# A fused attention and two-MoE kernel: key maxima of two batches by a GpSimd all-reduce, logits turned by transposes

## Chip, cores and metric

The kernel runs on one core of one Trainium2 chip. The metric is the device time of one execution in microseconds (us), from the core's own profile timestamps. Engines are named as in the profile: PE is TensorE (PEld its weight loads), DVE is VectorE, ACT is ScalarE, POOL is GpSimd, SP is the engine that issues most transfers. A name with q (POOLq) is an engine's own queue: instructions that steer and don't compute.

## What is computed

Linear attention with two softmaxes, then a gated MLP, then a mixture of eight experts weighted by an eight-step Sinkhorn iteration. Everything is in float32. The parts that the change touches are the second and third line of the first function (the maximum of k over the sequence) and the first line of the third.

```python
def attention(q, k, v):                    # 4 batches, 8 heads, 576 rows, 64 columns
    q_s = softmax(q, axis=-1)
    k_s = k - np.max(k, axis=2, keepdims=True)      # over the 576 rows of a head
    k_s = np.exp(k_s); k_s /= k_s.sum(axis=2, keepdims=True) + 1e-09
    kv = np.einsum('bhsd,bhse->bhde', k_s, v)
    return np.einsum('bhsd,bhde->bhse', q_s, kv)

def gated_mlp(x, w_gate, w_val, w_out, rms_g):      # 2304 x 512, inner width 1536
    xn = x / rms(x) * rms_g
    g = xn @ w_gate
    return (g * sigmoid(g) * (xn @ w_val)) @ w_out

def experts(x, w_gate, w1, w2):                     # 8 experts, inner width 1024
    logits = x @ w_gate; P = np.exp(logits - logits.max())
    for _ in range(8):
        P /= P.sum(1, keepdims=True) + 1e-9
        P /= P.sum(0, keepdims=True) + 1e-9
        P *= N / E
    return sum(P[:, e:e+1] * (np.maximum(x @ w1[e], 0) @ w2[e]) for e in range(E))
```

## The kernel before

Float32 products are split: each operand is a high part and a low part, and three matmuls (high with high, high with low, low with high) make one product. `mm3` (lines 786 to 790) issues them; the third, on line 790, reads the weight's low part, `w(1)`.

**Batches and ticks.** The attention of batch 0 is written out in `FIRST` (line 24). The attention of batches 1 to 3 is laid under the MLP products of the batch before: the loop at line 1974 goes over MLP blocks and batches, and in the first block (four slices f of the inner width) each batch b has 24 ticks. At a tick `att_do` issues the steps that the table `PLANS` (line 31) names for it. A negative tick of batch a is one of batch a-2's block: tick -5 of batch 2 is tick 19 of batch 0's block, -1 is its tick 23. Slice f has eight w_gate and w_val products, four ticks in all, and later four w_out products, two ticks. The w_out products of a slice come two slices behind the others (`LAG`), so the block of batch 0 ends with those of f=2 and f=3. There is no scheduler: every engine takes its instructions in the order in which the code issues them, and waits on semaphores.

**Weights of the MLP** are loaded raw and split by three steps, `split_a` to `split_c`, which a tick `s` in the table drives. The last of them copies the high part on ScalarE (line 370) and subtracts it on GpSimd (line 372) to get the low part; for the first twelve halves (`LO_POOL`) GpSimd does that. The last of these is the second half of w5, which is w_out of f=2 and f=3; the half itself is that of f=3. It is issued by the `s` of batch 1 at tick 20 of batch 0's block. The low half of each inner activation h is also made on GpSimd (line 837).

**Keys.** Steps `km` (`att_kmax`) take the maximum of a batch's keys over what lies in one partition, with three VectorE operations into `m1` (512 columns: 8 heads of 64). Step `mT` (`att_kmax2`) turns `m1` with four transposes and reduces it on VectorE, step `mb` (`att_kmax3`) turns the result back with four transposes of a broadcast column, so that a bank holds the maxima in every partition; ScalarE copies it to `m2`, which GpSimd reads. Steps `ks` subtract (VectorE for the main part, `G` for the 64-row tail on GpSimd), `ke` are exponentials on ScalarE, and `kv` is the product of keys and values, which begins with the tails. Steps `qm` take the query maxima on VectorE and subtract them on GpSimd (line 498), `qe` are their exponentials.

**Logits.** `logits` (line 875) leaves for each of four groups of 128 input columns eight rows of logits at partitions 32c to 32c+7 of a tile `lt`. `logits_out` (line 896) adds the four groups and turns them to token rows with one matmul a tile of 128 tokens against a 0/1 matrix `gather` (built once, line 2031), and copies the result to `probs`. There are 18 such tiles. The Sinkhorn iteration that follows uses GpSimd's `partition_all_reduce` nine times, on one and on eight columns (lines 914 and 931).

Of the kernel before, what the change touches and what calls it, by code (L numbers as in the profile page):

```python
# [7 lines left out]
F32 = mybir.dt.float32  # L8
# [4 lines left out]
ALU = mybir.AluOpType  # L13
AX = mybir.AxisListType
P = 128
# [37 lines left out]
    },  # L53
    2: {
        -6: "km_V_0 km_V_1",
        -4: "km_V_3",
        -3: "qm_0",
        -1: "mT",
        0: "qe_0",
        1: "mb ks_3_G qm_1 ks_0_V",  # L60
        2: "ke_0 ks_1_V ke_3 qT_0_0_V qT_0_1_V",
# [12 lines left out]
        22: "xT_2",  # L74
    },
    3: {
        -6: "qm_0 km_V_0",
        -5: "qm_1 km_V_1",
        -4: "km_V_3",
        -1: "mT",  # L80
        0: "mb qe_0",
        1: "ks_0_V",
        2: "ke_0 ks_3_G ks_1_V",
# [37 lines left out]
def kernel(  # L121
# [14 lines left out]
    nc = tc.nc  # L136
    B, H, S, D = q.shape
# [3 lines left out]
    E, _, F = moe2_w1.shape  # L141
    KC = DM // P
    HP = H // 2
# [19 lines left out]
    const = ctx.enter_context(tc.tile_pool(name="const", bufs=1))  # L163
# [14 lines left out]
    def psum(name):  # L178
        return pp.tile([P, 512], F32, tag="ps", name=name)

    ident = const.tile([P, P], F32, name="ident")
# [6 lines left out]
    for z in range(7):  # L188
        n = 1 << z
        nc.vector.tensor_scalar(  # L190
            out=ident[:, n : 2 * n], in0=ident[:, 0:n], scalar1=float(n), scalar2=None, op0=ALU.add
# [7 lines left out]
    probs = const.tile([P, NTILE, E], F32, name="probs")  # L199
# [2 lines left out]

    gcol = const.tile([P, KC], F32, name="gcol")

    gather = const.tile([P, E], F32, name="gather")
    xw = att[0]
    km, ms = (xp.tile([P, 1024], F32, tag=f"xt{z}", name=f"km{z}") for z in range(2))
    m1, m2 = (ms[:, z * 512 : (z + 1) * 512].rearrange("p (h d) -> p h d", h=H) for z in range(2))
# [166 lines left out]
    def split_tick():  # L375

        nb, nc_ = len(step_b), len(step_c)
        if nb:
            split_b()
        if nc_:  # L380
            split_c()
        if state["a"] < len(parts):
            if parts[state["a"]][0] < state["room"]:
                split_a()
        elif not nb and not nc_:
            pass_tick()
# [9 lines left out]
    kvn, kvd, rks, mxs, mbs = {}, {}, {}, {}, {}  # L396
# [11 lines left out]
            eng.tensor_tensor(out=m1[s, h], in0=m1[s, h], in1=ktl[s, g, h], op=ALU.max)  # L408

    def att_kmax2(b):  # L410
        mT = psum(f"mT{b}")
        for j in range(HP):
            nc.tensor.transpose(
                mT[:, j * P : (j + 1) * P], m1[:, 2 * j : 2 * j + 2, :].rearrange("p h d -> p (h d)"), ident
            )
        mxs[b] = mp.tile([P, HP], F32, tag="mx", name=f"mx{b}")
        nc.vector.tensor_reduce(
            out=mxs[b], in_=mT.rearrange("p (j s) -> p j s", j=HP), axis=AX.X, op=ALU.max
        )

    def att_kmax3(b):
        mb = psum(f"mb{b}")
        for j in range(HP):
            nc.tensor.transpose(mb[:, j * P : (j + 1) * P], mxs[b][:, j : j + 1].to_broadcast([P, P]), ident)
        mbs[b] = {nc.vector: mb.rearrange("p (h d) -> p h d", h=H).unsqueeze(2)}
        if b > 0:
            nc.scalar.copy(out=m2.rearrange("p h d -> p (h d)"), in_=mb)
            mbs[b][nc.gpsimd] = m2.unsqueeze(2)
        kvn[b] = vt[b].rearrange("p h u d -> p h (u d)")[:, :, DV : 3 * DV]
        rks[b] = mp.tile([P, H], F32, tag="rk", name=f"rk{b}")  # L430

# [360 lines left out]
    def ntok(b):  # L792
        return 512 if b < B else 256
# [46 lines left out]
    def m1_s2(f, b, h, py, first, last, tick):  # L840
        n = ntok(b)
        if f < BLOCKS[0][1]:
            split_until("o", f)
            w = wt["o", f - f % 2]
        else:
            pass_until(JOBS.index(("o", f - f % 2)) + 1)
            w = o_view(Wo[f - f % 2])
        for j in range(KC):
            mm3(
                py[j][:, 0:n],  # L850
                lambda z: w[:, z, f % 2, j * P : (j + 1) * P],
                None,
                None,
                [h[:, 0, 0:n], h[:, 1, 0:n]],
                n,
                first,
                last,
            )
            if j % 2:
                tick()  # L860
# [35 lines left out]
    def logits_out(b, pt=None):  # L896
        n = ntok(b)
        lt = lts.pop(b)
        if pt is None:
            pt = psum(f"lT{b}")  # L900
        m = n // P
        for i in range(m):
            nc.tensor.matmul(
                pt[:, i * E : (i + 1) * E], lhsT=lt[:, i * P : (i + 1) * P], rhs=gather, start=True, stop=True
            )
        nc.vector.tensor_copy(
            out=probs[:, 4 * b : 4 * b + m, :], in_=pt[:, 0 : m * E].rearrange("p (i e) -> p i e", e=E)
        )

    def sinkhorn():  # L910
# [37 lines left out]
    pt = {(p, name): dp.tile([P, 2048], F32, name=f"pt{p}{name}") for p in range(2) for name in ("T2", "T3", "T4")}  # L948
# [149 lines left out]
    def pass_tick():  # L1098

        k = state["job"]  # L1100
        if k >= min(state["jobs"], len(JOBS)):
            return
        job = JOBS[k]
        if k not in running:
            if job[0] != "t" and job not in job_raws:
                load_job(job)
                return
            after = lambda: load_job(JOBS[k + 1]) if k + 1 < len(JOBS) else None
            running[k] = (pair_sums if job[0] == "t" else convert)(job, after)
        if next(running[k], job) is job:  # L1110
            state["job"] += 1
# [862 lines left out]
    for t, (f0, f1) in enumerate(BLOCKS):  # L1974
        FT = f1 - f0
        for place, b in enumerate(range(NB) if t == 0 else (3, 2, 4)):

            now = {}
            if t == 0:
                state["tick"] = 0  # L1980
                for a, plan in PLANS.items():
                    for i, steps in plan.items():
                        i += 24 * (a - 1 - b)
                        if 0 <= i and (i < 24 or b == B - 1):
                            now[i] = now.get(i, []) + [(a, x) for x in steps.split()]

            def tick(now=now, t=t, b=b, place=place):
                for a, x in now.pop(state["tick"], ()):
                    att_do(a, x)
                state["tick"] += 1  # L1990
                if t == 0 and (b, state["tick"]) in GATES:
                    state["jobs"] = GATES[b, state["tick"]]
                if state["tick"] % 2 and not t == b == 0:
                    split_tick()
                elif EXTRA(t, b, place) and state["a"] == len(parts) and not step_b and not step_c:
                    pass_tick()

            pys = {}
            for fi in range(FT):
                f = f0 + fi  # L2000
                h = m1_s1(f, b, tick)

                def s2(f=f, b=b, h=h, fi=fi, t=t, pys=pys, tick=tick, FT=FT):
                    if fi == 0:
                        pys[0] = [psum(f"y{t}_{b}_{j}") for j in range(KC)]
                    m1_s2(f, b, h, pys[0], fi == 0, fi == FT - 1, tick)
                    if fi == FT - 1:
                        m1_evac(t, b, pys[0])

                queue.append(s2)  # L2010
                drain(LAG)
                if t == b == 0 and fi == 0:
                    load_kv(2)
                if t == b == 0 and fi == 2:
                    load_q(2, 0)
                    load_q(2, 4)
                if t > 0 and fi == 1:
                    state["jobs"] = ROOM[place]
                    if place == 0:
                        for name in ("T2", "T3", "T4"):  # L2020
                            recall_t(0, name)
            if t == 0 and b < B - 1:
                drain(0)
            if t == 0:
                assert not now, sorted(now)
                if b == 0:
                    load_q(3, 0)
                    load_q(3, 4)
                    load_kv(3)
                elif b == 2:  # L2030
                    nc.vector.tensor_reduce(
                        out=gather, in_=ident.rearrange("p (q e) -> p e q", e=E), axis=AX.X, op=ALU.add
                    )
                    state["room"] += 3
                    state["ahead"] = RAWS
                    for _ in range(RAWS - 2):
                        load_w()
# [61 lines left out]
    for z in range(2):  # L2099
        bank = psum(f"yt{z}")  # L2100
        for f in PASS:
            w = o_view(Wo[f - f % 2])
            s = slice((f - F0) * 256, (f - F0 + 1) * 256)
            for j in (0, 1):
                for i, (wz, hz) in enumerate(((0, 0), (0, 1), (1, 0))):
                    nc.tensor.matmul(
                        bank[:, j * 256 : (j + 1) * 256],
                        lhsT=w[:, wz, f % 2, (2 * z + j) * P : (2 * z + j + 1) * P],
                        rhs=h4[1 + hz][:, s],
                        start=(f == F0 and j == i == 0),  # L2110
                        stop=(f == F1 and i == 2),
# [123 lines left out]
    flat = [acc[b].rearrange("p a n -> p (a n)") for b in range(NB)]  # L2235
# [128 lines left out]
    for n in range(PER, last + 1):  # L2364
        g, e, u = units[n]
        start = n % PER == 0
# [89 lines left out]
```

## Time and profile before

| what | value |
|---|---|
| median of 3 runs | 1972.69 us (1972.36 to 1973.5) |
| profiled execution, its own time | 1972.83 us |
| its span, first to last instruction | 1971.0 us |
| instructions | 29247 |
| TensorE busy | 1947.1 us, 99% |
| VectorE busy | 1625.6 us, 82% |
| ScalarE busy | 830.0 us, 42% |
| GpSimd busy | 97.8 us, 5%, 100 instructions |
| moved by the transfer queues | 481.20 MB, mean 244 GB/s |

The attention and the first MLP block take the first 230 us or so, the logits stand near 470 and 532 us, and the rest is the experts. GpSimd works almost only in the first 280 us. In a row of a timeline the first column is the start, the second the length, and the brackets at its end tell how long the engine had been idle and what released it.

### The profile page before, as it was taken

How to read it: one execution, taken by the hardware profiler on the slowest of the kernel's cores; microseconds unless marked ns; L12 is line 12 of the kernel's file. 1: busy time of each engine (PE TensorE's matmuls, PEld its weight loads, DVE VectorE, ACT ScalarE, POOL GpSimd, SP SyncE). 2: the span in 40 equal slices, each digit the busy share in tenths (PEclk: the TensorE clock that was granted, in tenths of full speed). 3: DMA queues.
4: the chain of work that ended last, by engine and by line, in shares of the span. 5: the costliest groups of instructions: out<-in, count | busy, mean ns of one | idle time of the engine just before them, and what ended most of it. 6: DMA issues, size and time to landing. Idle time of an engine off the chain costs nothing.

```text
span 1971.0 us, 29247 instructions
## 1 busy us (share of the span) xinstructions
PE 1947.1 (99%) x10875; PEld 1810.7 (92%) x10875; DVE 1625.6 (82%) x3222; ACT 830.0 (42%) x1633; POOL 97.8 (5%) x100
## 2 busy tenths in 40 slices
PE   7899999999999999999999999999999999999999
PEld 6788888887888889999989999999999999999998
DVE  8868787755588877777778999999998989989898
ACT  5643545534355544455543333333343333333332
POOL 4521210000000000000000000000000000000000
PEclk9999999999999999999999999999999999999999
DMA  9401346587389777987787777667666767667663
GB/s 278 139 1 66 127 150 229 221 323 289 129 294 333 288 296 273 350 317 293 286 300 267 265 266 256 254 261 265 256 239 246 282 263 260 254 257 267 265 243 115
DMA packets 153974, 481.20 MB, mean 244 GB/s; under 512 B 17112, under 2 KB 81768, under 8 KB 149224
## 3 DMA queue, kind: packets, MB, share of 16 engines
q1 hardware_dynamic: 153304, 479.21, 66.7%
q8 instruction: 85, 1.39, 0.3%
q14 instruction: 57, 0.47, 0.1%
q10 hardware_dynamic: 528, 0.13, 0.0%
HBM read 334.65 MB, written 144.65 MB: 243 GB/s over the span
## 4 chain that ended last, share of the span: by engine, by line
PE 91%; DVE 4%; DMA 2%; ACT 1%; POOL 1%; issue 1%; SPq 1%; ACTq 0%; DVEq 0%; POOLq 0%
PE sb L1584 35%; PE sb L1830 13%; PE yb L1830 10%; PE yb L1619 4%; PE yb L1618 4%; PE yb L1617 4%; PE cx L1155 3%; PE cz L1155 2%; PE cy L1155 1%; PE ct L1230 1%; PE y L788 1%; PE y L790 1%; PE y L789 1%; PE pv L788 1%; PE pv L790 1%; PE pv L789 1%
## 5 line engine op out<-in xcount | busy, mean ns | idle before, releaser
L1584 PE MATMUL sb<-op1T,u 128*128 128x384 f32 x1536 | 298.4, 335 | 0.1
L1847 DVE TENSOR_TENSOR acc<-sb,acc 128x384 f32<-128x384 f32 x480 | 260.6, 557 | 27.4 <-PE sb L1830 23.2
L1584 PEld LDWEIGHTS sb<-op1T,u 128*128 128x128 f32 x1536 | 269.2, 188 | 1.1 <-DVE fx L1774 0.7
L1584 PE MATMUL sb<-op1B,u 128*128 128x384 f32 x1120 | 220.4, 335 | 0.0
L1584 PEld LDWEIGHTS sb<-op1B,u 128*128 128x128 f32 x1120 | 196.2, 188 | 0.9 <-DVE fx L1774 0.7
L1584 PE MATMUL sb<-op0T,u 128*128 128x384 f32 x768 | 149.6, 335 | 0.9 <-DVE cs L1659 0.9
L1584 PEld LDWEIGHTS sb<-op0T,u 128*128 128x128 f32 x768 | 135.6, 188 | 7.9 <-DVE cs L1659 2.5
L1774 DVE TENSOR_TENSOR fx<-mt,sb 128x384 f32<-128x384 f32 x128 | 71.0, 555 | 52.8 <-ACT mt L1778 31.2
L1584 PE MATMUL sb<-op0B,u 128*128 128x384 f32 x576 | 111.5, 336 | 0.0
L1584 PEld LDWEIGHTS sb<-op0B,u 128*128 128x128 f32 x576 | 101.5, 188 | 4.3 <-issue 1.7
L1830 PE MATMUL sb<-hc,u 128*128 128x384 f32 x504 | 104.6, 335 | 0.1
L1830 PE MATMUL sb<-hd,u 128*128 128x384 f32 x492 | 102.1, 334 | 0.1
L1830 PE MATMUL yb<-hd,u 128*128 128x384 f32 x426 | 96.7, 334 | 0.0
L1830 PEld LDWEIGHTS sb<-hc,u 128*128 128x128 f32 x504 | 88.7, 188 | 0.9 <-DVE acc L1847 0.6
L1830 PEld LDWEIGHTS sb<-hd,u 128*128 128x128 f32 x492 | 86.6, 188 | 0.7 <-ACT acc L1845 0.5
L1778 ACT COPY mt<-sb 128x384 f32<-128x384 f32 x64 | 30.8, 481 | 109.9 <-PE sb L1584 109.9
L1619 PE MATMUL yb<-u,hq 128*128 128x512 f32 x192 | 76.2, 397 | 0.3 <-DVE hq L1605 0.3
L1830 PEld LDWEIGHTS yb<-hd,u 128*128 128x128 f32 x426 | 75.9, 188 | 0.0
L1618 PE MATMUL yb<-u,hw 128*128 128x512 f32 x192 | 75.6, 394 | 0.0
L1619 PE MATMUL yb<-u,hw 128*128 128x512 f32 x192 | 75.6, 394 | 0.0
L1618 PE MATMUL yb<-u,hq 128*128 128x512 f32 x192 | 75.1, 391 | 0.0
L1729 DVE SCALAR_TENSOR_TENSOR fx<-fx,pb 128x384 f32<-128x384 f32 x128 | 71.3, 557 | 4.4
(479 smaller groups left out, 4387.6 us busy)
## 6 DMA issues: line engine op xcount, KB each, us to landing
u<-kept SPq DMA_DIRECT2D x256, 896.0 KB, 6.2
kept<-u SPq DMA_DIRECT2D x60, 896.0 KB, 5.9
kept<-u SPq DMA_DIRECT2D x58, 768.0 KB, 4.4
rw<-in_moe_w_dram SPq DMA_DIRECT2D x64, 512.0 KB, 5.9
pw<-w SPq DMA_DIRECT2D x12, 1024.0 KB, 5.0
w<-pw SPq DMA_DIRECT2D x12, 1024.0 KB, 7.1
kept<-u SPq DMA_DIRECT2D x58, 128.0 KB, 4.5
k<-in_k_dram SPq DMA_DIRECT2D x8, 512.0 KB, 5.0
```

The lines of the kernel that those rows point to most:

```text
L788: nc.tensor.matmul(o, lhsT=w(0), rhs=xb[0], start=first, stop=False)
L789: nc.tensor.matmul(o, lhsT=w(0), rhs=xb[1], start=False, stop=False)
L790: nc.tensor.matmul(o, lhsT=w(1), rhs=xb[0], start=False, stop=last)
L1155: nc.tensor.matmul(bank, lhsT=Wf[f][wz][:, at], rhs=block_x(p, xname, xz, c), start=(start and c == 0 and j == 0), stop=(c == 1 and j == 2 ...
L1584: nc.tensor.matmul(bank[:, 0:NT], lhsT=w[wz][:, WI[wname], c, :], rhs=x[xz][c], start=(start and c == 0 and j == 0), stop=(c == 1 and j == 2),
L1617: nc.tensor.matmul(py, lhsT=h[:, 0, s], rhs=w2[0][:, d], start=(u == 0 and f == 0), stop=False)
L1618: nc.tensor.matmul(py, lhsT=h[:, 0, s], rhs=w2[1][:, d], start=False, stop=False)
L1619: nc.tensor.matmul(py, lhsT=h[:, 1, s], rhs=w2[0][:, d], start=False, stop=(u == UE - 1 and f == 1))
L1729: nc.vector.scalar_tensor_tensor(out=fb[name], in0=c, scalar=0.0, in1=pbc[g, e][z], op0=ALU.max, op1=ALU.mult,)
L1774: add = lambda o, a, b: nc.vector.tensor_tensor(out=o, in0=a, in1=b, op=ALU.add)
L1830: nc.tensor.matmul(bank[:, 0:NT], lhsT=w[wz][:, d], rhs=h[:, hz], start=(start and k == 0), stop=True, skip_group_check=True)
L1847: nc.vector.tensor_tensor(out=a, in0=bank[:, 0:NT], in1=a, op=ALU.add)
```

## The change

For batches 2 and 3 the steps `mT` and `mb` no longer use TensorE: `mT` is one GpSimd instruction, `partition_all_reduce` with max over `m1`, whose result (in all partitions) goes to `m2`, and both VectorE and GpSimd subtract `m2`. The table moves `km` and `mT` of these batches to earlier ticks (the query maxima keep their ticks). The logits are turned by one transpose a tile, and VectorE adds the four groups while it evacuates. `gather` goes; a tile of the same size, of which one column is set to zero, takes its place. Batches 0 and 1 keep their transposes.

```diff
     2: {
         -6: "km_V_0 km_V_1",
-        -4: "km_V_3",
+        -5: "km_V_3 mT",
         -3: "qm_0",
-        -1: "mT",
...
     3: {
-        -6: "qm_0 km_V_0",
-        -5: "qm_1 km_V_1",
-        -4: "km_V_3",
-        -1: "mT",
+        -8: "km_V_0",
+        -7: "km_V_1",
+        -6: "qm_0 km_V_3 mT",
+        -5: "qm_1",
...
-    gather = const.tile([P, E], F32, name="gather")
+    fill_up = const.tile([P, 8], F32, name="fill_up")
+    nc.vector.memset(fill_up[:, 0:1], 0.0)
...
     def att_kmax2(b):
+        if b > 1:
+            flat = lambda t: t.rearrange("p h d -> p (h d)")
+            nc.gpsimd.partition_all_reduce(flat(m2), flat(m1), P, bass_isa.ReduceOp.max)
+            return
         mT = psum(f"mT{b}")
...
     def att_kmax3(b):
-        mb = psum(f"mb{b}")
-        for j in range(HP):
-            nc.tensor.transpose(mb[:, j * P : (j + 1) * P], mxs[b][:, j : j + 1].to_broadcast([P, P]), ident)
-        mbs[b] = {nc.vector: mb.rearrange("p (h d) -> p h d", h=H).unsqueeze(2)}
-        if b > 0:
-            nc.scalar.copy(out=m2.rearrange("p h d -> p (h d)"), in_=mb)
-            mbs[b][nc.gpsimd] = m2.unsqueeze(2)
+        if b > 1:
+            mbs[b] = {nc.vector: m2.unsqueeze(2), nc.gpsimd: m2.unsqueeze(2)}
+        else:
+            mb = psum(f"mb{b}")
+            for j in range(HP):
+                nc.tensor.transpose(mb[:, j * P : (j + 1) * P], mxs[b][:, j : j + 1].to_broadcast([P, P]), ident)
+            mbs[b] = {nc.vector: mb.rearrange("p (h d) -> p h d", h=H).unsqueeze(2)}
+            if b == 1:
+                nc.scalar.copy(out=m2.rearrange("p h d -> p (h d)"), in_=mb)
+                mbs[b][nc.gpsimd] = m2.unsqueeze(2)
...
         for i in range(m):
-            nc.tensor.matmul(
-                pt[:, i * E : (i + 1) * E], lhsT=lt[:, i * P : (i + 1) * P], rhs=gather, start=True, stop=True
-            )
-        nc.vector.tensor_copy(
-            out=probs[:, 4 * b : 4 * b + m, :], in_=pt[:, 0 : m * E].rearrange("p (i e) -> p i e", e=E)
+            nc.tensor.transpose(pt[:, i * P : (i + 1) * P], lt[:, i * P : (i + 1) * P], ident)
+        nc.vector.tensor_reduce(
+            out=probs[:, 4 * b : 4 * b + m, :],
+            in_=pt[:, 0 : m * P].rearrange("p (i c e) -> p i e c", c=KC, e=32)[:, :, 0:E],
+            axis=AX.X,
+            op=ALU.add,
         )
...
-                    nc.vector.tensor_reduce(
-                        out=gather, in_=ident.rearrange("p (q e) -> p e q", e=E), axis=AX.X, op=ALU.add
-                    )
```

Three places show how the order of instructions moves. The changed kernel's lines are numbered a few higher (372 stays, 498 is 505, 837 is 844, 442 is 449, 538 is 545).

GpSimd, end of batch 0's block, before. `h3_0` is the inner activation of f=3 of batch 0, `w5` the w_out weight of f=2 and f=3, `acc2` the queries of batch 2, `v3` the values of batch 3, `att1` the key tails, `km1` holds m1 and m2, `h0_1` is the activation of f=0 of batch 1.

```order
L837 TENSOR_TENSOR h3_0_888<-th3_0_832,h3_0_888 128x512
L372 TENSOR_TENSOR w5_686<-m5_1_723,w5_686 128x512
L498 TENSOR_TENSOR acc2_108<-acc2_108,qmx2_0_1008 128x8x128
L232 MEMSET v3_1084 128x16x2
L442 TENSOR_TENSOR att1_88<-att1_88,km1_114 64x512
L498 TENSOR_TENSOR acc2_108<-acc2_108,qmx2_1_1116 128x8x128
L837 TENSOR_TENSOR h0_1_1153<-th0_1_1120,h0_1_1153 128x512
```

The same place of the change:

```order
L844 TENSOR_TENSOR h3_0_889<-th3_0_833,h3_0_889 128x512
L413 ISA
L413 ISA km1_115<-km1_115 128x512
L372 ISA
L372 TENSOR_TENSOR w5_687<-m5_1_724,w5_687 128x512
L505 TENSOR_TENSOR acc2_108<-acc2_108,qmx2_0_1010 128x8x128
L232 MEMSET v3_1079 128x16x2
L449 TENSOR_TENSOR att1_88<-att1_88,km1_115 64x512
L505 TENSOR_TENSOR acc2_108<-acc2_108,qmx2_1_1105 128x8x128
L844 TENSOR_TENSOR h0_1_1142<-th0_1_1109,h0_1_1142 128x512
```

The all-reduce (the ISA row that names km1) stands with one unnamed instruction on either side between h3's low half and w5's.

GpSimd, end of batch 1's block, before. `acc3` are the queries of batch 3, `h0_2` is the activation of f=0 of batch 2.

```order
L837 TENSOR_TENSOR h3_1_1408<-th3_1_1387,h3_1_1408 128x512
L498 TENSOR_TENSOR acc3_109<-acc3_109,qmx3_0_1417 128x8x128
L498 TENSOR_TENSOR acc3_109<-acc3_109,qmx3_1_1436 128x8x128
L442 TENSOR_TENSOR att1_88<-att1_88,km1_114 64x512
L837 TENSOR_TENSOR h0_2_1563<-th0_2_1536,h0_2_1563 128x512
L471 MEMSET v3_1084 64x4x65 x4
```

The same place of the change:

```order
L844 TENSOR_TENSOR h3_1_1399<-th3_1_1376,h3_1_1399 128x512
L505 TENSOR_TENSOR acc3_109<-acc3_109,qmx3_0_1408 128x8x128
L413 ISA
L413 ISA km1_115<-km1_115 128x512
L505 ISA
L505 TENSOR_TENSOR acc3_109<-acc3_109,qmx3_1_1428 128x8x128
L449 TENSOR_TENSOR att1_88<-att1_88,km1_115 64x512
L844 TENSOR_TENSOR h0_2_1540<-th0_2_1513,h0_2_1540 128x512
L478 MEMSET v3_1079 64x4x65 x4
```

Here the three stand between the two query subtractions, ahead of the tail subtraction of the keys.

VectorE, end of batch 0's block, before. `att0` is the attention output of batch 1, `xp1` its banks, `km1` the key maxima of batch 2.

```order
L538 TENSOR_TENSOR att0_87<-xp1_1_1_940,rq1_1_1_944 128x3x2x64
L536 TENSOR_SCALAR rq1_1_2_962<-xp1_1_2_959 128x4
L537 RECIPROCAL rq1_1_2_962<-rq1_1_2_962 128x4
L538 TENSOR_TENSOR att0_87<-xp1_1_2_959,rq1_1_2_962 128x2x2x64
L408 TENSOR_TENSOR km1_114<-km1_114,att1_88 64x512
```

The same place of the change:

```order
L545 TENSOR_TENSOR att0_87<-xp1_1_1_941,rq1_1_1_945 128x3x2x64
L408 TENSOR_TENSOR km1_115<-km1_115,att1_88 64x512
L543 TENSOR_SCALAR rq1_1_2_965<-xp1_1_2_962 128x4
L544 RECIPROCAL rq1_1_2_965<-rq1_1_2_965 128x4
L545 TENSOR_TENSOR att0_87<-xp1_1_2_962,rq1_1_2_965 128x2x2x64
```

The last of the three key-maximum operations moves ahead of the last attention product's normalisation.

## Rows read from the trace of the kernel before

**Rows 1.** The page, part 1: each engine's busy time, share of the span, instructions.

```profile
PE 1947.1 (99%) x10875; PEld 1810.7 (92%) x10875; DVE 1625.6 (82%) x3222; ACT 830.0 (42%) x1633; POOL 97.8 (5%) x100
```

**Rows 2.** The page, part 4: shares of the chain that ended last.

```profile
PE 91%; DVE 4%; DMA 2%; ACT 1%; POOL 1%; issue 1%; SPq 1%; ACTq 0%; DVEq 0%; POOLq 0%
```

**Rows 3.** Stretches: us, then busy us (instructions) of PE, PEld, DVE, ACT, POOL; clock; DMA.

```profile
100.00:140.00 40.00, 40.00 (x291) 33.60 (x290) 27.31 (x65) 16.67 (x36) 12.81 (x11) 1.00 0.00 1
```

**Rows 4.** Line 740, first elementwise work on POOL: count, ns least/median/most, first and last start.

```profile
L740 POOLq MODIFY_POOL_CONFIG  x2: 25/25/25, 3.2 to 3.2; - x2
L740 POOLq EVENT_SEMAPHORE  x2: 17/30/43, 8.3 to 17.7; - x2
L740 POOL TENSOR_TENSOR acc<-acc,qmx_z x2: 1905/1906/1907, 13.5 to 18.3; 128x1024 f32<-128x1024 f32 x2
```

**Rows 5.** Line 914, first all-reduce (one column): same columns.

```profile
L914 POOLq MODIFY_POOL_CONFIG  x2: 8/8/8, 516.0 to 516.0; - x2
L914 POOL PARTITION_ALL_REDUCE gma<-gm x1: 381/381/381, 536.5 to 536.5; - x1
```

**Rows 6.** Line 931, the other all-reduces (eight columns): same columns.

```profile
L931 POOL PARTITION_ALL_REDUCE ca<-cs x8: 398/448/764, 551.8 to 633.3; - x8
```

**Rows 7.** TensorE's timeline, two pieces of batch 0's block: start us, us, instruction.

```profile
59.07 0.50 PE L790 MATMUL y<-h,w 128*128 128x512 f32 x1 [0.85 <-POOL w L372]
...
85.17 0.40 PE L790 MATMUL y<-h,w 128*128 128x512 f32 x1
```

**Rows 8.** GpSimd's timeline, end of batch 0's block.

```profile
77.11 1.28 POOL L837 TENSOR_TENSOR h<-th,h 128x512 fp32r<-128x512 f32 x1 [2.91 <-ACT h L836]
80.66 1.29 POOL L372 TENSOR_TENSOR w<-m,w 128x512 fp32r<-128x512 f32 x1 [2.26 <-ACT w L370]
```

**Rows 9.** VectorE's timeline, end of batch 0's block.

```profile
81.67 0.56 DVE L538 TENSOR_TENSOR att<-xp,rq 128x384 f32<-128x384 f32 x1
...
83.49 0.67 DVE L408 TENSOR_TENSOR km<-km,att 64x512 f32<-64x512 f32 x1
```

**Rows 10.** GpSimd's timeline, end of batch 1's block.

```profile
127.37 2.89 POOL L498 TENSOR_TENSOR acc<-acc,qmx 128x1024 f32<-128x1024 f32 x1
...
138.23 1.30 POOL L442 TENSOR_TENSOR att<-att,km 64x512 f32<-64x512 f32 x1 [4.18 <-ACT km L427]
```

**Rows 11.** ScalarE's timeline, begin of batch 2's block.

```profile
140.46 0.61 ACT L446 ACTIVATE att<-att 64x512 f32<-64x512 f32 x1
143.46 0.62 ACT L836 CAST h<-th 128x512 fp32r<-128x512 f32 x1 [2.38 <-DVE th L834]
143.99 1.05 ACT L446 ACTIVATE k<-k 128x1024 f32<-128x1024 f32 x1
```

**Rows 12.** TensorE's timeline, the key-value product of batch 3.

```profile
145.26 0.69 PE L460 MATMUL kv<-att,att 128*64 128x66 f32 x16
```

**Rows 13.** TensorE's timeline, the first 33 us.

```profile
5.23 6.42 PE L781 MATMUL cold<-att 128*128 128x128 f32 x32 [0.71 <-DVE att L216]
...
25.38 2.25 PE L527 MATMUL xp<-v,qT 128*128 128x130 f32 x18 [2.60 <-DVE att L538]
27.46 5.08 PE L783 MATMUL cold<-ident 128*128 128x128 f32 x45
```

**Rows 14.** TensorE's timeline: on either side of mT's transposes; the logits' gather matmuls, the next.

```profile
134.86 0.39 PE L790 MATMUL y<-h,w 128*128 128x512 f32 x1
...
135.77 0.39 PE L789 MATMUL pg<-x,w 128*128 128x512 f32 x1
...
468.26 0.95 PE L903 MATMUL lT<-gather,lt 128*128 128x8 f32 x8
469.07 0.72 PE L1155 MATMUL cx<-p1T,w 128*128 128x512 f32 x2
```

**Rows 15.** TensorE's waits between 40 and 190 us: us in total, times, longest.

```profile
PE kv L460 <- ACT k L446: 0.3, 1, 0.3
...
PE mT L413 <- DVE x L571: 0.3, 1, 0.3
```

## Prediction

> **What bounds the kernel now.** I read the page first: TensorE is busy 99% of the span, VectorE 82%, GpSimd 5% [rows 1], and the chain that ended last is TensorE for 91% [rows 2]. So the time goes up or down by what TensorE itself is given to do, or is made to wait; work saved on VectorE or ScalarE is worth nothing unless TensorE waited for it. The table by stretches says the same of the place of the change: between 100 and 140 us TensorE is busy 40.00 of 40 us while GpSimd has 12.81 us of work [rows 3]. That stretch has no slack in which a stall could be won back, so a stall of TensorE there is added to the end in full. Then I followed GpSimd's timeline, since the change puts three things into its queue, and asked at each place who waits behind them.
>
> **What comes in.** GpSimd's order shows for each of batches 2 and 3 an all-reduce over 512 columns with an unnamed instruction ahead of it and one behind it. The trace names that instruction: MODIFY_POOL_CONFIG, a change of the code that GpSimd's cores run. Before, it stands once ahead of the first elementwise instruction [rows 4] and once ahead of the first all-reduce [rows 5]. The change adds four: to the all-reduce's code and back, twice.
>
> *Price of one code change, S.* Nothing shows it by itself, since both old ones lie under other waits. Below, nothing excludes 0. Above: the first one was issued at 3.2 us, the queue's next record (a semaphore for a transfer) stands at 8.3, the first elementwise instruction at 13.5 [rows 4]. So S is at most 5.1 us if loading holds the queue, and at most 10.3 us if it does not. I take 6.0: nearer the queue's own record than the other, since the instruction at 13.5 was held by VectorE. The Trainium skill, "GPSIMD Engine Reference", section "Instruction dispatch", puts the first call after such a change at about 6 us (5.95 measured), a price no row here shows by itself; with it the sum would come out 0.4 us lower.
>
> *Price of the all-reduce, X.* The one over a single column took 0.381 us [rows 5], the eight over 8 columns 0.398 to 0.764, median 0.448 [rows 6]. A line through 0.381 and the fastest gives 2.4 ns a column, so 512 columns take 1.6 us; through the median 9.6 ns a column and 5.3 us. I take 3.5, between them. The outer ends are 0.38 (columns free) and 64 times the median, 28.7 us (all of it proportional).
>
> **Batch 2: the first stall.** In GpSimd's queue the three stand ahead of the low half of w5 (line 372), which stood right behind the low half of h3 before. That half of w5 is the weight of the third matmul of the last w_out product of batch 0 (f=3, z=1): the L790 that starts at 85.17 [rows 7]. Before, it was written from 80.66 to 81.95 [rows 8] and TensorE did not wait. That TensorE does wait for just this kind of write is on record: at 59.07 an L790 stood 0.85 us for a line-372 write [rows 7]. Now: h3's half ends at 77.11 + 1.28 = 78.4 [rows 8]; code change until 84.4; the key maxima are ready before that, for the tail maximum (L408, 0.67 us) now follows at once on the product that ends at 81.67 + 0.56 = 82.2 [rows 9], so at 82.9; all-reduce until 87.9; code change back until 93.9; w5's half 1.29 us more, 95.2. TensorE goes on at about 95.25 instead of 85.17: **10.1 us**. In general 2S + X - 5.4. Queued behind w5's half on GpSimd are the subtraction of query half 0, a memset and the tail subtraction of batch 2. TensorE's clients of these come after the stalled matmul, so they shift with it, and they end earlier relative to it than before. The value load that waits for that memset (SP) starts later too, but its reader is 40 us away.
>
> **Batch 3: the second stall.** The three stand between the two query subtractions. The first one began at 127.37 and took 2.89 us [rows 10], so the way back ends at 130.3 + 2S + X = 145.8. Then the second query subtraction, 1.9 us as this shape takes undisturbed [rows 4]: 147.7; the tail subtraction, 1.30 [rows 10]: 149.0. Behind it ScalarE, which works in order: tail exponential 0.61, cast of h 0.62, key exponential 1.05, about 2.2 us with their overlap [rows 11]: 151.2. The key-value product needs both exponentials and started at 145.26 [rows 12]: **5.9 us** of waiting; in general 2S + X - 9.6. VectorE's first key subtraction waits for m2 until 130.3 + 6.0 + 3.5 = 139.8, where it began at 138.2 with the tail subtraction [rows 10]; that 1.6 us lies inside the longer wait and costs nothing more.
>
> **The clock.** Ahead of its first long run TensorE ran at half rate: 32 matmuls of 128 columns took 6.42 us, where later 45 took 5.08 (0.113 each, so 3.6 for 32) [rows 13]. That is a loss of 2.8 us at 1.2 against 2.4 GHz. After an idle of 2.60 us the next 18 of 130 columns took 2.25, 0.125 each: full rate kept [rows 13]. A stall of 10.1 us lies far above that one, 5.9 nearer. So I put 2.8 for the first and half of it, 1.4, for the second: **4.2 us**, between 0 and 5.6. The Trainium skill, "TensorE: Matmul & The Clock Gate", section "HAM oscillation — how this bites in real kernels", lets waits for operands bring the array back to half rate again and again; by it the term would be 5.6, and no wait of this trace is long enough to show it.
>
> **What goes out.** Four sets of four transposes (mT and mb, twice). One set stands between an L790 at 134.86 and an L789 two matmuls later at 135.77: 0.91 us, where two steps take 0.46, so 0.45 us each [rows 14], 1.8 together. With them go 0.26 us of waiting ahead of the first mT and 0.3 ahead of a key-value product [rows 15], 0.5. VectorE's two maxima and ScalarE's two copies go as well; they lie under TensorE's work and count for nothing. The logits: four gather matmuls (eight passes) fill 468.26 to 469.07, 0.81 us [rows 14]; four transposes fill 0.45. With 18 tiles that is 4.5 times 0.36, 1.6 us. VectorE's reduction in place of the copy is a little longer, and nobody stands behind it. The removed gather sum on VectorE, and the added memset of one column, count nothing. Gain: **3.9 us**.
>
> **Sum.** 10.1 + 5.9 + 4.2 - 3.9 = 16.3 us. The profiled execution took 1972.83 us (span 1971.0), 0.14 above the median of the runs, 1972.69. So I expect **1989 us**, 0.8% slower. With S from 4.5 to 7.5 and X from 2 to 5, 2S + X goes from 11 to 20: stalls of 5.6 + 1.4 to 14.6 + 10.4, the clock 1 to 5, so +4 to +26 us, 1977 to 1999.
>
> **Rivals.**
> - *The code change is cheap and the stalls are not there.* With 2S + X under 5.4 (S under about 1 us) nothing waits and the gain is left: 1972.8 - 3.9 = 1969 us. For it: the first old change shows no instruction longer than 25 ns [rows 4]. Against it: the queue's next record is 5.1 us off. The point from which it decides between faster and slower is 2S + X = 9.3, where the first stall eats the gain. Chance 0.12.
> - *Only the way out costs, the way back does not*, the old code being still there. Then S counts once: 6.0 + 3.5 - 5.4 = 4.1 us of first stall, none of the second, against 3.9: 1973 us, 1975 with some clock. For it: the trace never shows a change back. Against it: the order has the same instruction on the way back. Chance 0.08.
> - *The all-reduce goes by columns.* X = 28.7: stalls 35.3 and 31.1, clock 5.6, minus 3.9: 2041 us. Against it: 8 columns hardly took longer than 1 [rows 5, 6]. The Trainium skill, "GPSIMD Engine Reference", section "Cross-partition — where GPSIMD wins", has a GpSimd reduction over partitions at 247.7 us for 2048 columns; at that rate 512 columns would be an estimated 62 us and the time near 2110. Its rate would make 8 columns about 1 us, and the trace has half of that, so I give this whole rival 0.05.
>
> **How the numbers follow.** The forecast has 0.75. Range 1973 to 2001: it holds the forecast's case with a little of its tails and the rival that pays one way; left out are the cheap case, the costly all-reduce and the ends, some 0.2. A measurement of this kernel can tell about 0.2% from no change, 3.9 us: 1968.7 to 1976.6. The cheap case lies on that bound, half and half: faster 0.06; same 0.06 of it, 0.07 of the one-way case and 0.02 of the forecast's low tail, 0.15; slower 0.79.
>
> **What would show it.** Right: in TensorE's waits a wait of some 10 us of y L797 (the old L790) for GpSimd's w, line 372, near 85 us; one of some 6 us ahead of the key-value product of batch 3, put down to ScalarE's exponential; on GpSimd an all-reduce near 84 us and 12 us in which it runs nothing around it; matmuls at half rate behind the first stall. In the logits four transposes where eight passes stood. Wrong: GpSimd's w5 half ending before 86 us, or TensorE's stall there being under 4 us; then S is far smaller. A stall over 20 us would say that X is.

## The result and the profile after

The changed kernel took 1987.67 us, median of 4 runs (1985.91 to 1988.64), against 1973.05 us of the kernel before beside it (4 runs, 1972.36 to 1973.5): ratio 1.0073, 95% interval 1.0061 to 1.0085, 14.6 us slower. The forecast was 1989, slower. The profiled execution of after is the run of 1985.91 us, with a span of 1984.1 us, 13.1 over that of before; the trace explains those 13.1.

The page of after, part 1 and the engines' shares of the chain, against [rows 1, 2]:

```profile
PE 1946.4 (98%) x10841; PEld 1809.9 (91%) x10841; DVE 1625.4 (82%) x3220; ACT 828.7 (42%) x1631; POOL 101.2 (5%) x102
...
PE 90%; DVE 4%; ACT 1%; issue 1%; DMA 1%; POOL 0%; ACTq 0%; SPq 0%; DVEq 0%; POOLq 0%
```

TensorE has less work by 0.7 us and the span is 13.1 us longer, so TensorE waits. Its waits in after between 40 and 220 us (us in total, times, longest), where before had nothing over 1.7 us:

```profile
PE y L797 <- POOL w L372: 10.1, 2, 9.2
PE kv L467 <- ACT att L453: 5.8, 1, 5.8
...
PE kv L467 <- ACT k L453: 0.3, 1, 0.3
...
PE pg L795 <- DVE x L578: 0.3, 1, 0.3
```

The first two are the stalls that were forecast, at the forecast places (line 790 of before is 797 now, 460 is 467). The 10.1 is two waits: the stall of 9.2 and the old wait of [rows 7]; that it equals the forecast 10.1 is chance. The two of 0.3 are the waits of [rows 15]: the second stands ahead of a w_gate matmul now, where mT's transposes stood. GpSimd's timeline of after shows what made them; its rows of before are [rows 8, 10]:

```profile
76.03 1.28 POOL L844 TENSOR_TENSOR h<-th,h 128x512 fp32r<-128x512 f32 x1 [2.92 <-ACT h L843]
83.50 1.80 POOL L413 PARTITION_ALL_REDUCE km<-km  x1 [6.19 <-DVE att L545]
92.16 1.25 POOL L372 TENSOR_TENSOR w<-m,w 128x512 fp32r<-128x512 f32 x1 [6.85 <-issue]
...
136.74 1.29 POOL L844 TENSOR_TENSOR h<-th,h 128x512 fp32r<-128x512 f32 x1 [8.75 <-ACT h L843]
137.99 2.36 POOL L505 TENSOR_TENSOR acc<-acc,qmx 128x1024 f32<-128x1024 f32 x1
146.29 1.80 POOL L413 PARTITION_ALL_REDUCE km<-km  x1 [5.95 <-DVE acc L876]
155.16 1.89 POOL L505 TENSOR_TENSOR acc<-acc,qmx 128x1024 f32<-128x1024 f32 x1 [7.07 <-issue]
157.02 1.25 POOL L449 TENSOR_TENSOR att<-att,km 64x512 f32<-64x512 f32 x1
```

Around each all-reduce GpSimd runs nothing for 6 us before and 7 us behind. The brackets name VectorE as what the all-reduce waited for; that is the profile's guess at the last event. VectorE had ended the key maxima at 81.75. What filled the time is the code change, whose record is here (all-reduce's line in after):

```profile
L413 POOLq MODIFY_POOL_CONFIG  x4: 6/8/11, 77.5 to 140.6; - x4
L413 POOL PARTITION_ALL_REDUCE km<-km x2: 1802/1802/1803, 83.5 to 146.3; - x2
```

From the record at 77.5 to the all-reduce at 83.5 are 6.0 us; from the all-reduce's end at 85.3 to the half of w5 at 92.16 are 6.9. The second pair is 5.7 and 7.1.

TensorE's timeline of after at the first stall:

```profile
83.85 0.39 PE L796 MATMUL y<-h,w 128*128 128x512 f32 x1
93.46 0.79 PE L797 MATMUL y<-h,w 128*128 128x512 f32 x1 [9.22 <-POOL w L372]
94.05 0.63 PE L795 MATMUL y<-h,w 128*128 128x512 f32 x1
...
97.37 0.40 PE L797 MATMUL y<-h,w 128*128 128x512 f32 x1
```

The matmul behind the half of w5 (92.16 + 1.25 = 93.41) starts at 93.46. The next ones take 0.63 us and not 0.40, until about 97. The stretches of after show why (us; busy us and instructions of PE, PEld, DVE, ACT, POOL; granted clock; transfers):

```profile
92.00:96.00 4.00, 2.54 (x16) 1.65 (x20) 0.00 (x0) 0.00 (x0) 3.84 (x4) 0.50 0.00 0
96.00:100.00 4.00, 4.00 (x34) 3.22 (x26) 0.35 (x1) 2.76 (x10) 0.56 (x1) 0.85 0.51 157
100.00:104.00 4.00, 3.75 (x18) 2.94 (x17) 4.00 (x6) 4.00 (x8) 0.42 (x1) 1.00 1.15 337
...
158.00:162.00 4.00, 3.01 (x52) 2.94 (x54) 0.14 (x1) 3.52 (x5) 1.55 (x2) 0.50 0.01 4
162.00:166.00 4.00, 4.00 (x48) 3.39 (x45) 3.39 (x14) 0.00 (x0) 1.24 (x4) 1.00 0.00 0
```

Granted clock 0.50, that is 1.2 GHz, behind both stalls. The second stall in TensorE's timeline of after, against [rows 12]:

```profile
158.99 1.15 PE L467 MATMUL kv<-att,att 128*64 128x66 f32 x16 [5.75 <-ACT att L453]
159.93 3.09 PE L467 MATMUL kv<-v,k 128*64 128x65 f32 x64
```

The 16 tail matmuls take 1.15 us where they took 0.69.

**The balance.** The same TensorE instruction stands in both traces; its start after, less its start before, tells how much has been lost up to it.

| instruction | before | after | difference | step |
|---|---|---|---|---|
| w_out matmul ahead of the place | 79.15 | 78.08 | -1.07 | |
| third matmul with w5's half | 85.17 | 93.46 | +8.29 | stall 9.4 |
| second matmul, end of half rate | 87.11 | 97.08 | +9.97 | half rate 1.7 |
| w_out, behind batch 2's old sets | 130.44 | 139.31 | +8.87 | given back 1.1 |
| w_gate, behind batch 3's old sets | 138.53 | 146.46 | +7.93 | given back 0.9 |
| key-value product, tails | 145.26 | 158.99 | +13.73 | stall 5.8 |
| first w_val matmul behind it | 147.74 | 162.95 | +15.21 | half rate 1.5 |
| first logits' turn | 468.26 | 483.24 | +14.98 | |
| expert product after the first ten tiles | 494.38 | 508.83 | +14.45 | logits -1.2, a wait +0.7 |
| end of span | 1971.0 | 1984.1 | +13.1 | logits -0.8, rest |

The -1.07 at the top is hardly the change: all that stands ahead of it is one memset of 0.06 us on VectorE (the tile in the place of `gather`). The warm-up matmuls of [rows 13] went from 0.42 to 0.27 us each at 8.4 us in this execution and at 10.7 in that of before, which is the clock's first rise. With the memset their run took 5.29 to 6.62 us in the traces kept here, without it 6.42 and 5.29, so the memset doesn't decide it.

### The profile page after: what moved, and what is told of

Read it like the earlier page. It is cut to its first block, busy times and chain, and to the rows that moved or that the text cites. A ratio compares the mean times of both kernels' runs of the same rounds, so it can differ in the third digit from the quotient of the medians.

```text
span 1984.1 us, 29179 instructions
## 1 busy us (share of the span) xinstructions
PE 1946.4 (98%) x10841; PEld 1809.9 (91%) x10841; DVE 1625.4 (82%) x3220; ACT 828.7 (42%) x1631; POOL 101.2 (5%) x102
## 3 DMA queue, kind: packets, MB, share of 16 engines
q8 instruction: 85, 1.39, 0.3%
## 4 chain that ended last, share of the span: by engine, by line
PE 90%; DVE 4%; ACT 1%; issue 1%; DMA 1%; POOL 0%; ACTq 0%; SPq 0%; DVEq 0%
PE sb L1592 35%; PE sb L1838 13%; PE yb L1838 10%; PE yb L1627 4%; PE yb L1626 4%; PE yb L1625 4%; PE cx L1163 3%; PE cz L1163 2%; PE cy L1163 1%; PE ct L1238 1%; PE y L797 1%; PE y L795 1%; PE y L796 1%; PE pv L795 1%; PE pv L797 1%
```

## Experiments

The logits alone, w5's half, batch 3's early place and the five pieces were measured against 22 runs of the kernel before (median 1972.77 us), the others against 21 (1972.56). Diffs are against the changed kernel, except where said.

**Logits alone.** The key maxima of batches 2 and 3 go back to transposes, with the old table.

```diff
-        if b > 1:
+        if b > 3:
...
-            if b == 1:
+            if b > 0:
```

> Only the logits' transposes are in; keys as in the kernel before. Theory: TensorE saves 0.4 us for each set of four tiles (about 2 us in all), and 0.7 us of it is given back at a wait for VectorE near 494 us, so about 1.4 us faster, 1971.6 us, with four transposes spanning some 0.36 us where eight passes spanned 0.81. Rival: the longer reduction on VectorE (0.29 against 0.19 us) costs as much as TensorE saves: 1973 us or more.

1970.87 us (11 runs, 1969.37 to 1971.75), ratio 0.9990 (0.9981 to 0.9999): 1.9 us faster than before, barely clear of no change. The whole loss comes from the maxima; the logits' part is no loss.

**The half of w5 to VectorE.** What TensorE waited for in the first stall leaves GpSimd's queue; the three instructions stay.

```diff
-LO_POOL = {0, 1, 2, 3, 4, 5, 6, 7, 8, 9, 10, 11}
+LO_POOL = {0, 1, 2, 3, 4, 5, 6, 7, 8, 9, 10}
```

> The change, but the low half of w5 for f=3 is made on VectorE, so that no weight stands behind the code changes on GpSimd. Theory (the first stall is the queue's order): the wait of 9.2 us at L797 and its half-rate stretch (1.7 us) go, VectorE pays 0.7 us that is hidden, ScalarE's query exponential waits some 1 us: about 1976.5 us, and the second stall of 5.8 us stays. Rival (the wait moves on to the next reader of GpSimd, the key-value product of batch 2): a new wait of 5 us or more there, and 1982 us or more.

1978.30 us (10 runs, 1976.74 to 1980.94), ratio 1.0031 (1.0022 to 1.0040): 9.4 us less than the changed kernel. TensorE's waits of this kernel:

```profile
PE kv L467 <- ACT att L453: 5.7, 1, 5.7
...
PE qTp L513 <- ACT acc L508: 1.0, 1, 1.0
PE y L797 <- POOL w L372: 0.8, 1, 0.8
```

The first stall is gone, the second stands as it was. The 0.8 is the old wait of [rows 7]. A new wait of 1.0 us appears: the query subtraction behind the all-reduce is what comes late next. The expectation had named ScalarE's late exponential, but added no wait of TensorE for it; the time is 1.8 us above the expected one. The granted clock stays 1.00 from 84 to 100 us.

**Batch 3's all-reduce early.** It moves to a place on GpSimd where TensorE needs nothing behind it for long; the first stays.

```diff
-        -8: "km_V_0",
-        -7: "km_V_1",
-        -6: "qm_0 km_V_3 mT",
+        -16: "km_V_0 km_V_1",
+        -15: "km_V_3 mT",
+        -6: "qm_0",
```

> The change, but batch 3's key maxima and all-reduce come nine ticks earlier, between the low halves of h1 and h2 of batch 1. Theory: tail subtraction and second query subtraction are no longer behind the code changes, so the wait of 5.8 us ahead of batch 3's key-value product and its half-rate stretch (1.5 us) go, and h2 is ready in time: about 1980.3 us; the first stall stays. Rival: the wait moves to h2 or h3 (w_out products of batch 1 waiting for GpSimd, 3 us or more), or the three VectorE operations delay the attention products: 1984 us or more.

1979.24 us (5 runs, 1978.06 to 1981.22), ratio 1.0034 (1.0021 to 1.0046): 8.4 us less. The second stall is gone (of the key-value product only the old 0.3 is left), the first is 9.0. GpSimd's timeline of this kernel still has the code changes at full length:

```profile
125.08 1.80 POOL L413 PARTITION_ALL_REDUCE km<-km  x1 [6.01 <-DVE rq L543]
133.96 2.68 POOL L844 TENSOR_TENSOR h<-th,h 128x512 fp32r<-128x512 f32 x2 [7.07 <-issue]
```

Two halves of h are made late there, one behind the other, and no wait of TensorE answers to it.

**Both moves together.**

> The change with both moves: w5's last low half on VectorE, and batch 3's all-reduce nine ticks earlier. Theory (the two stalls are all that the change costs): both go, what is left of the price is a wait of 1 us of a query transpose for ScalarE and some 0.5 us for tail operands, and TensorE keeps the eight sets of transposes and passes that went: about 1971 us, 1.5 to 2.5 us below the kernel before. Rival: each move alone still carries a loss that the other's stall covered, and the time stays at 1974 us or more.

1969.68 us (11 runs, 1968.78 to 1972.44), ratio 0.9987 (0.9978 to 0.9996), 2.9 us faster than before. Of new waits of TensorE 0.4 us is left, behind the query subtraction. The two stalls add up (9.4 and 8.4 us gained by the single moves, 18.0 by both) and are the whole loss.

**The all-reduce in five pieces.** Same work, cut by columns.

```diff
-            nc.gpsimd.partition_all_reduce(flat(m2), flat(m1), P, bass_isa.ReduceOp.max)
+            for c0, c1 in ((0, 256), (256, 384), (384, 448), (448, 480), (480, 512)):
+                nc.gpsimd.partition_all_reduce(flat(m2)[:, c0:c1], flat(m1)[:, c0:c1], P, bass_isa.ReduceOp.max)
```

> Each all-reduce of 512 columns is cut into 256, 128, 64, 32 and 32. Theory (0.37 us and 2.8 ns a column): 1.09, 0.73, 0.55, 0.46, 0.46 us, and both stalls grow by 1.5 us, about 1990.7 us. Rival (a cost that steps, or depends little on columns below some size): the pieces of 32 and 64 take the same time, or more than 0.7 us each. The code changes stay at about 6 us out and 6.9 us back in either case.

1990.26 us (one run). GpSimd's timeline of this kernel:

```profile
84.02 3.13 POOL L414 PARTITION_ALL_REDUCE km<-km  x5 [5.91 <-DVE att L546]
94.23 1.25 POOL L372 TENSOR_TENSOR w<-m,w 128x512 fp32r<-128x512 f32 x1 [7.09 <-issue]
```

The pieces of 256, 128, 64, 32 and 32 columns took 1.09, 0.79, 0.60, 0.51 and 0.51 us. With 1.80 for 512 and 0.381 for one [rows 5], a call costs about 0.38 us and 2.8 ns a column. Five pieces still pay one code change out and one back (5.9 and 7.1): the large price is that of the change between kinds of work, where four more calls add 1.3 us. The waits grew to 10.5 and 7.6 us; one run tells no more than the direction of the time.

**One column instead of 512.** In the kernel before, an all-reduce over one column of batch 2's maxima, whose result nobody reads, is put at the place of the changed kernel's first one.

```diff
-        -4: "km_V_3",
+        -5: "km_V_3 one",
...
+        elif name == "one":
+            nc.gpsimd.partition_all_reduce(spare1, m1[:, 0, 0:1], P, bass_isa.ReduceOp.max)
```

> The kernel before with one all-reduce of a single column added at batch 2's place, its result unused (so key maxima and logits go as before). Theory (the two code changes, 6.0 and 6.9 us, make the stall; the reduction itself adds 1.8 us): L790 waits 9.2 - 1.4 = 7.8 us and loses some 1.6 us at half rate: about 1982.3 us. Rival (the reduction over 512 columns makes it): a wait under 2 us, 1974 us.

1982.76 us (2 runs), ratio 1.0053 (1.0034 to 1.0071), 10.2 us over before. GpSimd's and then TensorE's timeline of this kernel:

```profile
85.08 0.38 POOL L714 PARTITION_ALL_REDUCE spare<-km  x1 [5.88 <-DVE att L539]
92.08 1.25 POOL L373 TENSOR_TENSOR w<-m,w 128x512 fp32r<-128x512 f32 x1 [6.62 <-issue]
```

```profile
93.38 0.79 PE L793 MATMUL y<-h,w 128*128 128x512 f32 x1 [7.26 <-POOL w L373]
```

A reduction of 0.38 us brings a stall of 7.26 us. Of the 14.7 us that the changed kernel's first all-reduce takes with its two code changes, the reduction is 1.8.

**Keeping TensorE busy in the first stall.** 76 transposes of the identity that nobody reads run while it waits; the stall itself stays.

```diff
+                    if t == b == 0 and fi == 3:
+                        warm_up(9, 76)
```

> The change, with 76 transposes of the identity into a spare bank (8.3 us of work that nobody reads) ahead of the last w_out product of batch 0, so that TensorE is busy in most of the first stall. Theory (the slow matmuls behind the stall are the clock): the granted clock stays at 1.0 around 90 us, L797 starts when it did, and the 1.7 us behind it are saved: about 1986 us. Rival (they are slow for another reason, as contention in memory, or TensorE's clock falls all the same): no gain, 1987.7 us or more.

1984.49 us (4 runs, 1984.17 to 1985.03), ratio 1.0062 (1.0048 to 1.0076). TensorE's timeline and the stretches of this kernel:

```profile
84.06 8.52 PE L790 MATMUL cold<-ident 128*128 128x128 f32 x76
...
94.00 0.50 PE L797 MATMUL y<-h,w 128*128 128x512 f32 x1 [0.95 <-POOL w L372]
94.33 0.40 PE L795 MATMUL y<-h,w 128*128 128x512 f32 x1
```

```profile
92.00:96.00 4.00, 3.05 (x29) 1.96 (x28) 0.00 (x0) 0.16 (x1) 3.31 (x4) 1.00 0.00 0
```

The clock stays at 1.00 where it was 0.50, and the matmuls behind the stall take 0.40 where they took 0.63. So the half rate is the stall's doing, a cost beside the wait. The time fell 3.2 us below the changed kernel's median where the trace accounts for 1.7; the changed kernel's four runs lie 2.7 us apart and were taken beside other runs of before, so the other 1.5 is not settled.

**Only batch 3 by the all-reduce, early.** Batch 2 keeps its transposes, and the logits are turned by transposes: the version that the others point to.

```diff
-        if b > 1:
+        if b > 2:
...
+        -16: "km_V_0 km_V_1",
+        -15: "km_V_3 mT",
+        -6: "qm_0",
```

> Only batch 3 uses the all-reduce, at its early place between the low halves of h1 and h2; batch 2 keeps its transposes; the logits are turned by transposes. Theory: no wait for GpSimd at all, 0.9 us of transposes gone besides what the logits save (1.9 us in their own run): about 1970 us. Rival: h2's low half, which comes after the code change back, is late and a w_out product of batch 1 waits 2 us or more: 1972 us or more.

1968.86 us (11 runs, 1968.42 to 1970.99), ratio 0.9984 (0.9975 to 0.9992): 3.7 us faster than before and 18.8 faster than the changed kernel. Its interval overlaps that of both moves together, so which of these two is better is open. GpSimd's timeline of this kernel shows the same hole, 15 us long, without a victim on TensorE:

```profile
108.86 1.29 POOL L845 TENSOR_TENSOR h<-th,h 128x512 fp32r<-128x512 f32 x1 [4.38 <-ACT h L844]
115.96 1.80 POOL L414 PARTITION_ALL_REDUCE km<-km  x1 [5.80 <-DVE th L836]
125.17 2.55 POOL L845 TENSOR_TENSOR h<-th,h 128x512 fp32r<-128x512 f32 x2 [7.41 <-issue]
```

## Why the prediction was right

**The bound and the mechanism: right.** TensorE had no slack, and what it was made to wait for came out at the end. Both stalls stand at their places; removing the cause of each removed that stall and left the other, and removing both gave the gain.

**Price of a code change, 6.0: right on the way out, low on the way back.** It took 6.0 and 5.7 out, 6.9 and 7.1 back. The Trainium skill, "GPSIMD Engine Reference", section "Instruction dispatch", puts the first call after such a change at about 6 us; the way out agrees (5.7 to 6.0 us), the way back is about 1 us dearer here. With 5.95 the sum would have come out 0.2 us lower, where the prediction says 0.4, for S enters it four times. Its bound of 5.1 us, taken from the queue's next record [rows 4], was no bound: every change measured here took longer. The rivals of a cheap change and of a free way back fall with these rows.

**Price of the all-reduce, 3.5: mis-sized, it took 1.80.** The line through one column and the fastest of the eight-column calls gave 1.6 and was the better one; the slower eight-column calls were no measure of columns. The rival of a cost by columns falls: 512 columns cost 4.7 times one column. The Trainium skill, "GPSIMD Engine Reference", section "Cross-partition — where GPSIMD wins", has its 247.7 us for another operation (`tensor_reduce` along the partitions); the 62 us estimated from it do not carry over, and the measured 1.80 decides.

The two errors nearly cancel: 2S + X was 15.5, and measured it is 6.0 + 1.8 + 6.9 = 14.7.

**First stall, 10.1: right in kind, 9.4 by the balance.** The formula 2S + X - 5.4 gives 9.3 with the measured 14.7.

**Second stall, 5.9: measured 5.8, but by four errors that cancel.** The code changes and the reduction took 14.8, 0.7 less than assumed. The tail exponential alone frees the key-value product, since that begins with the tails: 158.27 to 158.99 is 0.7 us where 2.2 stood, 1.5 less. On the other side, the first query subtraction ended 1.2 us later than TensorE's own delay of 8.87 explains (130.26 to 140.35, 10.1). VectorE's timeline of after tells from where:

```profile
131.40 0.69 DVE L835 SCALAR_TENSOR_TENSOR th<-th,pg 128x512 f32<-128x512 f32 x1 [0.63 <-ACT th L834]
132.01 1.22 DVE L404 TENSOR_TENSOR km<-k 128x1024 f32<-128x1024 f32 x1
133.14 1.67 DVE L665 TENSOR_SCALAR att<-att,ry 128x512 f32<-128x512 f32 x4
134.73 0.68 DVE L406 TENSOR_TENSOR km<-km 128x512 f32<-128x512 f32 x1
135.33 0.68 DVE L841 TENSOR_TENSOR th<-th,pv 128x512 f32<-128x512 f32 x1
```

The key maxima moved to earlier ticks now stand ahead of the product that h is made of (it was at 124.72 before), which comes 10.6 us late and not 8.9; h's half on GpSimd follows it, and the all-reduce follows that. The prediction did not count this moved step. And batch 3's two removed sets (0.9) lie ahead of the stall: TensorE reaches the key-value product sooner and waits that much longer. Together -0.7 - 1.5 + 1.2 + 0.9 is -0.1.

**Clock, 4.2: mis-sized, 1.7 + 1.5 = 3.2.** That both stalls bring half rate was right, for the second more surely than was said. Each cost less, for TensorE ran at half rate only for 3.6 us (93.46 to 97.1) and 3 us (158.99 to 162) behind it. The price taken from the start of the kernel (2.8) is that of a longer run at half rate. The Trainium skill, "TensorE: Matmul & The Clock Gate", section "HAM oscillation — how this bites in real kernels", which lets such waits bring the array back to half rate each time, agrees in kind: 0.50 behind both.

The other row that the prediction leaned on, full rate kept behind a wait of 2.60 us [rows 13], was that of one execution. In the trace of after the same wait is followed by half rate (TensorE's timeline, then a stretch):

```profile
24.30 3.11 PE L534 MATMUL xp<-v,qT 128*128 128x130 f32 x18 [2.58 <-DVE att L545]
27.20 5.92 PE L790 MATMUL cold<-ident 128*128 128x128 f32 x45
```

```profile
25.00:27.00 2.00, 2.00 (x14) 2.00 (x14) 1.86 (x8) 1.06 (x3) 1.28 (x1) 0.63 1.09 362
```

So that row was no safe case to set the 5.9 us against. Here the slow stretch cost nothing at the end, for right behind these matmuls TensorE had waited 1.39 us for VectorE in before, and in after it does not.

**What goes out, 3.9: mis-sized in its parts, 3.4 by the balance.** The four sets gave 2.0 where 1.8 were counted, but neither of the two waits (0.5) went: both 0.3 still stand in TensorE's waits of after. And batch 3's half of the sets went into the second stall, as above. The logits: four transposes took 0.35 us and not 0.45, in TensorE's timeline of after:

```profile
483.24 0.60 PE L910 MATMUL lT<-ident,lt 128*128 128x128 f32 x4
483.59 1.64 PE L1163 MATMUL cx<-p1T,w 128*128 128x512 f32 x6
...
508.83 1.66 PE L1163 MATMUL cx<-p1T,w 128*128 128x512 f32 x6 [0.87 <-DVE c L1211]
```

So a group of four saved 0.81 - 0.35 = 0.46 us, and 18 tiles 2.0 (1.2 near 470, 0.8 near 532). The wait for VectorE in the last line was 0.21 before; it and what stands around it give 0.7 of this back. That nobody stands behind VectorE there was thus not quite so. What the reduction (0.29 us for the copy's 0.19) has to do with that wait is open: it is 0.8 us in the kernel with the logits alone, 2.0 in the one with only batch 3, and missing in the one with unread transposes, all with the same logits.

**Sum.** 9.4 + 5.8 + 3.2 - 3.4 is 14.9 before rounding, from the place on, less 1.1 with which this execution led and less 0.7 in drifts outside the steps: the 13.1 of the span.

## What to carry to other kernels

An all-reduce on GpSimd between elementwise work costs two code changes, some 13 us of that engine in this kernel, even for one column: put it where nothing that the bounding engine needs within that time stands behind it in the queue, and group such calls. Follow the queue to the first reader of what stands behind it, for that is where the price falls; and ahead of a wait, work saved on the waiting engine only lengthens the wait.

## What was not expected of the hardware

- The way back to the elementwise code is dearer than the way out in every trace: 6.6 to 7.6 us from the all-reduce's end to the next instruction, against 5.6 to 6.0 from the record of the change to the all-reduce.
- The all-reduce over 128 partitions is cheap for its columns: 0.38 us for one column, 1.80 for 512, both well under one code change.
- The stalls of 9.22, 7.26 and 5.75 us all ended at half rate. The wait of about 2.6 us in the warm-up did in some executions only: in nine traces with a wait of 2.58 to 2.61 us the granted clock fell behind it in three. In the kernel with 76 unread transposes it stayed at 1.00 though w5's half came as late as in the changed kernel.
- The first rise of the clock came at different times in different executions of nearly the same opening code (8.4 and 10.7 us in the two traces compared here). In these two it goes with a lead of 1.07 us at 79 us, the size of some gains sought here.
